# Bias of the first tiles summed ahead of their scores, masks made early, and a third buffer for the late loads

## The chip, the cores and the metric

The kernel runs on one core of a Trainium2 chip. The time is the device time of one execution in microseconds (us). A profile taken with an execution has a span, which is some 2 us shorter than the time. Most executions of one kernel agree within 0.3%; a few fall in a slower state, and those are left out of every ratio below. The verdict "same" means a difference of less than 2%. Where the text says faster or slower, it means only that the 95% interval of the ratio leaves out 1.

## The reference, cut to what matters

Attention with a local window and a few global keys, and behind it a layer with a squared ReLU:

```python
B, H, S, D = 4, 8, 768, 64            # 24 tiles of 128 rows
scores = q @ k.T / sqrt(D) + bias     # bias = -slope[h] * distance
keep   = (key < 8) | (0 <= row - key < 96)
a      = softmax(where(keep, scores, -1e9))
x      = (a @ v)                      # 3072 x 512 in all
out    = relu(x @ w_in) ** 2 @ w_out  # 512 -> 2048 -> 512
```

## The kernel before

It goes through 24 tiles of 128 rows. A tile's query and key are transposed (`tr`, copied to `qkT`), multiplied to scores (`sc`), put through exp on ScalarE (`at`), multiplied with the values (`po`), divided by the row sums to `x`, and transposed again (`trx`, copied to `xT`). Two tiles make a block of 256 rows; for each block come eight steps of `hT` (x @ w_in), ReLU and square, and `acc` (the product with w_out). For tiles from 6 on, SyncE's transposing DMAs take the place of `tr` and `trx`. A planner in the kernel's source simulates the engines with assumed durations and fixes the order of all instructions when the kernel is built; each engine then works through its own instructions in that order.

Three parts matter here. The first loads, on the queue of GpSimd, and the constants on VectorE:

```python
load_part(0, 1)                                   # q of tile 1
nc.gpsimd.iota(pbi, ...)                          # key minus row
load_part(1, 1); load_v(0); load_v(1)
# ...
nc.vector.tensor_tensor(out=pb, in0=pbt, in1=pbw, op=Alu.min)     # the bias
for h in range(H):
    nc.vector.tensor_scalar_mul(sid[h], ident, float(slopes[h] / scale))
def emit_pb0(e):                                  # the bias with global keys
    nc.vector.tensor_copy(pb0, pb[:, 0, :])
    nc.vector.tensor_scalar_max(pb0[:n_global, :], pb0[:n_global, :], float(-n_local))
# ...
for w in "i0 T2 i1 T3 i2 o0 i3 o1 i4 o2 T4 i5 o3 i6 o4 T5 i7 o5 o6 o7".split():
    ...                # T: q, k, v of a tile; i, o: a slice of w_in, of w_out
```

For tiles 0 to 2 the bias is added on TensorE: the scores open a sum, and a product of a scaled identity `sid` with `pb` closes it:

```python
for ...: nc.tensor.matmul(out=sc[odd, g][:, at, :], lhsT=qkT[...], rhs=qkT[...],
                          start=(odd, g) not in opened, stop=False)
for ...: nc.tensor.matmul(out=sc[odd, g][:, at, :], lhsT=sid[2 * pair + odd],
                          rhs=pb0 if first else pb[:, kt, :], start=False, stop=True)
```

The loads of tiles 6 to 23 ("late") share NQ = 2 buffers. GpSimd waits with each until the transpose out of the buffer is done.

Of the kernel before, what the change touches and what calls it, by code (L numbers as in the profile page):

```python
# [21 lines left out]
class Plan:  # L22
# [9 lines left out]
    LAG = {"PE": 0.25, "ACT": 0.15, "DVE": 0.12, "SP": 2.6, "POOLQ": 0.8, "DMAQ": 1.2, "DMA": 0.0}  # L32
# [67 lines left out]
def kernel(  # L100
# [11 lines left out]
    nc = tc.nc  # L112
# [26 lines left out]
    NQ, NKT = 2, 2 * TPB  # L139
# [31 lines left out]
    LEADS = {6: 10, 7: 10}  # L171
    NHS = 14
    E_AT = 14.0
    NWARM = 8
    LEAD = 12
# [65 lines left out]
    for j in range(NFIRST + 2):  # L241
        nc.vector.memset(v_sb[j][:, :, D : D + 1], 1.0)
    load_part(0, 1)
    nc.gpsimd.iota(pbi, pattern=[[-P, 2], [-1, P]], base=0, channel_multiplier=1)  # L244
    issue[0] += 0.4
# [9 lines left out]
    nc.vector.tensor_scalar(ident32, pbi[:, 0, :], 0.0, None, op0=Alu.is_equal)  # L255
    nc.vector.tensor_scalar(ident, pbi[:, 0, :], 0.0, None, op0=Alu.is_equal)
# [7 lines left out]
    )  # L264
    nc.vector.tensor_tensor(out=pb, in0=pbt, in1=pbw, op=Alu.min)
    for h in range(H):
        nc.vector.tensor_scalar_mul(sid[h], ident, float(slopes[h] / scale))

    def emit_pb0(e):
        nc.vector.tensor_copy(pb0, pb[:, 0, :])  # L270
        nc.vector.tensor_scalar_max(
            pb0[:n_global, :], pb0[:n_global, :], float(-n_local)
        )
        nc.vector.memset(pb[:n_global, 1, :], float(-n_local))

    pb_op = plan.op(("pb",), {"DVE": 0.75}, emit_pb0, key=-40.0)

    def emit_ones(e, js):
        for j in js:
            nc.vector.memset(v_sb[j][:, :, D : D + 1], 1.0)  # L280
# [22 lines left out]
    def any_copy(e, dst, src):  # L303
        if e == "ACT":
            nc.scalar.copy(dst, src)  # L305
        else:
            nc.vector.tensor_copy(dst, src)  # L307

    maskE = [
        plan.op(  # L310
            ("E", odd, g), {"ACT": 0.8}, key=0.3 + 2 * g + odd, ready=E_AT,
            emit=lambda e, odd=odd, g=g: [
                nc.scalar.activation(
                    E[:, odd, g, i], pb, Act.Exp, scale=float(slopes[4 * g + 2 * i + odd])
                )
                for i in range(2)
            ],
        )
        for g in range(2)
        for odd in range(2)  # L320
    ]

    def emit_E0(e, odd):
# [8 lines left out]
            ("E0", odd), {"DVE": 0.6}, emit=lambda e, odd=odd: emit_E0(e, odd), key=9 + odd,  # L332
            deps=[maskE[odd], maskE[2 + odd]],
# [7 lines left out]
    xT_op = {}  # L341
    xT_of = {}
# [3 lines left out]
    for j in range(NT):  # L346
# [6 lines left out]
        if j in late:  # L353
            def emit_load(e, j=j):
                load_tile(j)
            ld = plan.op(
                ("load", j), {"POOLQ": 2.6}, emit_load, deps=qk_users[slot(j)] + [ones[j]],
                key=base, ready=issue[0],
            )
            qk_users[slot(j)] = []  # L360
            ld = plan.op(("data", j), {"DMAQ": 2.7}, None, deps=[ld], key=base)
            land["q", j] = land["k", j] = land["v", j] = ld
# [6 lines left out]
        for n in range(2) if j < JQK else ():  # L369
            users = []  # L370

            def emit_tr(e, j=j, n=n, fp=fp):
                tr = ps_g.tile([P, NPAIR, P], FP32 if fp else BF16, name="tr", tag="g")
                src = plain[n, j] if fp else qk_ring[slot(j)][:, n, :]
                for pair in range(NPAIR):
                    nc.tensor.transpose(  # L376
                        out=tr[:, pair, :], in_=src[:, pair * P : (pair + 1) * P],
                        identity=ident32 if fp else ident,
                    )
                tiles["tr", n, j] = tr  # L380

            tr = plan.op(
                ("tr", n, j), {"PE": 0.5 if fp else 0.24}, emit_tr,
                deps=[land["qk"[n], j]], key=base, takes=(*G, [users]),
            )

            def emit_T(e, j=j, n=n, T_=T_):
                any_copy(e, T_[:, n], tiles.pop(("tr", n, j)))

            c = plan.op(  # L390
                ("T", n, j), {"DVE": 0.7 if fp else 0.43, "ACT": 0.57}, emit_T,
                deps=[tr] + ku, key=base + 0.1,
            )
            users += [tr, c]
            parts.append(c)
            if not fp:
                qk_users[slot(j)].append(tr)
        if j >= JQK:
            def emit_dT(e, j=j, T_=T_):
                nc.sync.dma_start_transpose(  # L400
                    out=T_.rearrange("p n a c -> p (n a) c"),
                    in_=qk_ring[slot(j)].rearrange("p n c -> p (n c)"),
                )

            T = plan.op(
                ("T", j), {"SP": 2.0}, emit_dT,
                deps=[land["q", j], land["k", j], xT_op[j - 3]] + ku, key=base - 6,
            )
            qk_users[slot(j)].append(T)
            parts = [T]  # L410
# [8 lines left out]
        def emit_sc(e, gs, j=j, first=first):  # L419
            sc = {}  # L420
            for g in gs:
                for odd in range(2):
                    sc[odd, g] = ps_g.tile([P, 4, P], FP32, name="sc", tag="g")
                    tiles["sc", j, odd, g] = sc[odd, g]
            todo = [
# [4 lines left out]
            todo = [x for x in todo if x[0] in gs]  # L430
            opened = set()
            for g, pair, at, kt in todo:
                for odd in range(2):
                    half = slice(odd * D, (odd + 1) * D)
                    nc.tensor.matmul(  # L435
                        out=sc[odd, g][:, at, :],
                        lhsT=qkT[(j - kt) % NKT][half, 1, pair, :],
                        rhs=qkT[j % NKT][half, 0, pair, :],

                        start=j >= NBIAS or (odd, g) not in opened,  # L440
                        stop=j >= NBIAS,
                        skip_group_check=True,
                    )
                    opened.add((odd, g))
            for g, pair, at, kt in todo if j < NBIAS else ():
                for odd in range(2):
                    nc.tensor.matmul(
                        out=sc[odd, g][:, at, :],
                        lhsT=sid[2 * pair + odd],
                        rhs=pb0 if first else pb[:, kt, :],  # L450
                        start=False,
                        stop=True,
                        skip_group_check=True,
                    )

        deps = list(parts)
        if j < NBIAS:
            deps.append(pb_op)
# [3 lines left out]
        for gs in [(0,), (1,)] if j < NSPLIT and not first else [tuple(range(groups))]:  # L462
            n = 8 * len(gs)
            o = plan.op(
                ("sc", j, gs[0]), {"PE": 0.25 + 0.029 * n + (0.056 * n if j < NBIAS else 0)},
                lambda e, gs=gs, f=emit_sc: f(e, gs), deps=deps, key=base + 1 + 2 * gs[0],
                takes=(*G, busers[2 * gs[0] : 2 * gs[-1] + 2]),
            )
            ku.append(o)
# [3 lines left out]
        for g in range(groups):  # L473
            for odd in range(2):
# [3 lines left out]
                def emit_exp(e, j=j, odd=odd, g=g):  # L478
# [11 lines left out]
                    ("exp", j, odd, g), {"ACT": 0.58}, emit_exp, deps=[s_[g]],  # L490
# [3 lines left out]
                users += [s_[g], x_]  # L494
# [6 lines left out]
                def emit_mul(e, j=j, odd=odd, g=g, first=first):  # L501
# [10 lines left out]
                    ("mul", j, odd, g), vec(0.38), emit_mul,  # L512
                    deps=[x_, maskE0[odd] if first else maskE[2 * g + odd]],
# [8 lines left out]
        if 1 <= t < TPB - 1:  # L522
            def emit_gk(e, j=j, t=t):
# [5 lines left out]
                ("gk", j), vec(0.17), emit_gk, deps=list(s_.values()), key=base + 4  # L529
# [7 lines left out]
        for hf in range(2):  # L537
# [34 lines left out]
            def emit_norm(e, j=j, hf=hf):  # L572
# [13 lines left out]
                ("norm", j, hf), vec(0.6), emit_norm,  # L586
# [6 lines left out]
        if 1 <= t < TPB - 1:  # L593
            def emit_gv(e, j=j, t=t):
# [3 lines left out]
                ("gv", j), vec(0.28), emit_gv, deps=[p_, norm[1]], key=base + 5  # L598
# [7 lines left out]
        if j < JX:  # L606
# [23 lines left out]
            c = plan.op(("xT", j), {"DVE": 0.43, "ACT": 0.57}, emit_xT, deps=[f_], key=base + 5.1, takes=xT_ring)  # L630
            users += [f_, c]
            xusers.append(f_)
        else:
# [8 lines left out]
            c = plan.op(("xT", j), {"SP": 1.3}, emit_xT, deps=norm, key=base + 5, takes=xT_ring)  # L642
# [4 lines left out]
        if tt == 1:  # L647
            c["deps"].append(xT_op[j - 1])
# [5 lines left out]
    for n, (blk, s) in enumerate(order1):  # L654
# [31 lines left out]
        r = plan.op(("relu", blk, s), {"ACT": 0.58}, emit_relu, deps=[a], key=n + 0.5, takes=("hr", 2, [rusers]))  # L686
# [10 lines left out]
        d = plan.op(("sq", blk, s), vec(0.68), emit_sq, deps=[r], key=n + 1.0, takes=("hs", NHS, [husers]))  # L697
# [11 lines left out]
    for blk in range(NBLK):  # L709
# [9 lines left out]
        for s, sub, half in order2:  # L719
# [29 lines left out]
            if s == NSTEP - 1:  # L749
                ousers = []  # L750

                def emit_o(e, blk=blk, sub=sub, half=half, cols=cols):
                    o_sb = work.tile([P, d_model], FP32, name="o", tag="o", bufs=4)
# [4 lines left out]
                    ("o", blk, sub), {"ACT": 0.57, "DVE": 0.62} if half is None else {"ACT": 0.37},  # L758
                    emit_o, deps=[o], key=8 * blk + s + 1.0, takes=("o", 4, [ousers]),
# [4 lines left out]
                def emit_st(e, blk=blk, sub=sub, half=half, cols=cols):  # L764
# [5 lines left out]

                st = plan.op(
                    ("st", blk, sub), {"SP": 0.4}, emit_st, deps=[ev],
                    key=8 * blk + s + 9.0,
                )
                ousers.append(st)

    for o in plan.run({"PE": 4.2, "DVE": 4.4, "ACT": 4.2, "DMAQ": issue[1]}):
# [37 lines left out]
```

## Time and profile before

| | before |
|---|---|
| time, fast runs | 215.96 us (215.77 to 216.22) |
| span | 213.9 us |
| TensorE busy, its weight loads | 96%, 66% |
| first real matmul, end of the last | 4.58, 210.80 us |
| last slice of w_in landed | 37.3 us |

TensorE's busy share hides what is lost, because the records of pipelined matmuls overlap. I use one measure throughout, the **stall**: at a moment t, t less 4.4 us less the work started by then, where each matmul counts as its distance between starts (0.109 us for hT, 0.2155 for acc, and so on, as in the prediction), and 4.4 us is a fixed point shortly before the first of them. The matmuls are counted by the starts of their weight loads, because in some traces 31 or 32 of the 1992 matmul records are missing and no weight load is. A stall that grows by 0.5 us between two moments means that TensorE lost 0.5 us there. Before, it stands at 1.47 us at 10 us, 3.68 at 18, 6.40 at 30 and 9.24 at 200: two thirds of what is lost is lost in the first 30 us.

### The profile page before, as it was taken

To read this page: it belongs to the slowest core of one execution; us is meant where nothing else is said; L and a number is where in the kernel's file an instruction comes from. 1 tells how busy PE (TensorE), PEld (TensorE's weight loads), DVE (VectorE), ACT (ScalarE), POOL (GpSimd) and SP (SyncE) were. 2 spreads that over 40 slices of the span, in tenths; PEclk is the share of its full clock that TensorE was granted. 3 is DMA by queue.
4 is the path that set the end of the run, shared out by engine and by line. 5 is a ranking of instruction groups with operands and counts; after the bars stand their busy time and mean duration, and the time that the engine had idled before them with its cause. 6 is when DMAs were issued, how large, how long until landed. Compare 5 with 4: busy or idle time off the path is not lost.

```text
span 213.9 us, 5031 instructions
## 1 busy us (share of the span) xinstructions
PE 206.2 (96%) x1992; PEld 141.8 (66%) x1992; DVE 141.9 (66%) x366; ACT 118.7 (55%) x218; POOL 74.1 (35%) x91
## 2 busy tenths in 40 slices
PE   7889899999999999999999999999999999999994
PEld 3676567657667767766767767666767767766773
DVE  5377948736688767756868768756867767744540
ACT  2698575714574845743845745743845745734441
POOL 7997577309044350418043143226113000000000
PEclk9999999999999999999999999999999999999999
DMA  9999999999999999999969969999989910310202
GB/s 129 150 164 200 179 196 183 175 209 111 162 199 116 228 129 93 171 138 111 198 85 91 183 118 95 167 124 109 184 128 82 174 26 3 123 25 3 98 0 98
DMA packets 113702, 27.58 MB, mean 129 GB/s; under 512 B 104336, under 2 KB 110736, under 8 KB 113680
## 3 DMA queue, kind: packets, MB, share of 16 engines
q0 software_dynamic: 79200, 13.37, 82.8%
q1 hardware_dynamic: 34480, 13.90, 32.9%
q8 instruction: 15, 0.25, 0.5%
q14 instruction: 7, 0.06, 0.1%
HBM read 27.26 MB, written 6.29 MB: 157 GB/s over the span
## 4 chain that ended last, share of the span: by engine, by line
PE 86%; DMA 7%; POOL 4%; issue 1%; DVE 0%; ACT 0%; POOLq 0%
PE hT L661 38%; PE acc L731 38%; PE sc L435 5%; PE po L550 5%; DMA win<-in_moe_w_in_dram 4%; DMA qk<-in_k_dram 3%; POOL qk L193 2%; POOL v L193 2%; POOL win L193 1%; PE tr L376 0%; PE trx L613 0%; DVE x L578 0%; ACT o L305 0%; POOL pbi L244 0%; DVE v L595 0%
## 5 line engine op out<-in xcount | busy, mean ns | idle before, releaser
L661 PE MATMUL hT<-xT,win 128*128 128x256 bf16 x768 | 99.0, 273 | 0.5 <-DMA win<-in_moe_w_in_dram 0.3
L731 PE MATMUL acc<-wout,hs 128*128 128x512 bf16 (+1 forms) x400 | 95.6, 370 | 0.7 <-DMA wout<-in_moe_w_out_dram 0.7
L682 ACT ACTIVATE hr<-hT 128x512 f32<-128x512 f32 x96 | 57.3, 598 | 60.5 <-PE hT L661 58.9
L661 PEld LDWEIGHTS <-win 128*128 128x128 bf16 x768 | 71.0, 98 | 18.2 <-DMA win<-in_moe_w_in_dram 1.1
L694 DVE TENSOR_TENSOR hs<-hr 128x512 bf16<-128x512 f32 x96 | 65.0, 689 | 24.9 <-ACT hr L682 24.1
L731 PEld LDWEIGHTS <-hs 128*128 128x128 bf16 x400 | 38.4, 98 | 28.5 <-issue 0.8
L483 ACT ACTIVATE esc<-sc 128x512 bf16<-128x512 f32 x78 | 42.6, 598 | 13.2 <-PE sc L435 13.1
L193 POOL DMA_DIRECT2D qk<-in_q_dram x23 | 20.6, 897 | 82.5 <-DMA qkT<-qk 79.5
L508 DVE TENSOR_TENSOR at<-esc,E 128x512 bf16<-128x512 bf16 x78 | 32.4, 420 | 6.8 <-ACT esc L483 5.8
L193 POOL DMA_DIRECT2D v<-in_v_dram x24 | 21.6, 901 | 2.2 <-DVE at L508 1.2
L578 DVE TENSOR_TENSOR x<-po,rs 128x256 bf16<-128x256 f32 x48 | 20.4, 424 | 1.7
L193 POOL DMA_DIRECT2D qk<-in_k_dram x23 | 20.6, 897 | 0.2 <-issue 0.2
L550 PEld LDWEIGHTS <-at 128*128 128x128 bf16 x352 | 16.7, 98 | 5.8 <-ACT at L483 0.4
L550 PE MATMUL po<-v,at 128*128 128x65 bf16 x352 | 18.7, 193 | 0.3 <-ACT at L483 0.3
L435 PEld LDWEIGHTS <-qkT 64*128 64x128 bf16 x352 | 9.9, 94 | 9.9 <-issue 8.3
L577 DVE RECIPROCAL rs<-po 128x4 f32<-128x4 f32 x48 | 8.6, 179 | 10.2 <-PE po L550 10.2
L435 PE MATMUL sc<-qkT 64*128 64x128 bf16 x192 | 13.2, 219 | 1.0 <-DVE qkT L307 0.5
L305 ACT COPY o<-acc 128x512 f32<-128x512 f32 (+1 forms) x14 | 7.8, 557 | 9.2 <-PE acc L731 9.2
L307 DVE COPY o<-acc 128x512 f32<-128x512 f32 x11 | 7.6, 691 | 6.1 <-PE acc L731 6.1
L435 PE MATMUL sc<-qkT,qkT 64*128 64x128 bf16 x160 | 11.4, 216 | 0.0
L524 DVE COPY qkT<-qkT 128x32 bf16<-128x32 bf16 x16 | 3.8, 235 | 7.4 <-PE sc L435 7.3
L193 POOL DMA_DIRECT2D win<-in_moe_w_in_dram x8 | 6.7, 840 | 0.6 <-DMA wout<-in_moe_w_out_dram 0.6
(40 smaller groups left out, 61.3 us busy)
## 6 DMA issues: line engine op xcount, KB each, us to landing
out_dram<-o SPq DMA_DIRECT2D x23, 256.0 KB, 4.1
v<-in_v_dram POOLq DMA_DIRECT2D x24, 128.0 KB, 6.0
qk<-in_q_dram POOLq DMA_DIRECT2D x23, 128.0 KB, 4.5
qk<-in_k_dram POOLq DMA_DIRECT2D x23, 128.0 KB, 5.4
win<-in_moe_w_in_dram POOLq DMA_DIRECT2D x8, 256.0 KB, 8.1
wout<-in_moe_w_out_dram POOLq DMA_DIRECT2D x8, 256.0 KB, 8.9
qkT<-qk SPq DMA_TRANSPOSE x18, 5.1
xT<-x SPq DMA_TRANSPOSE x18, 3.5
```

The costliest lines, as they stand in the source:

```text
L193: nc.gpsimd.dma_start(out=dst, in_=src)
L305: nc.scalar.copy(dst, src)
L435: nc.tensor.matmul(out=sc[odd, g][:, at, :], lhsT=qkT[(j - kt) % NKT][half, 1, pair, :], rhs=qkT[j % NKT][half, 0, pair, :],  start=j >= N ...
L483: nc.scalar.activation(out=esc, in_=tiles.pop(("sc", j, odd, g)).rearrange("p a c -> p (a c)"), func=Act.Exp, scale=scale,)
L508: nc.vector.tensor_mul(at, tiles.pop(("esc", j, odd, g)), bias)
L550: nc.tensor.matmul(out=po[:, hi, :], lhsT=tiles["at", j, odd, g][:, at * P : (at + 1) * P], rhs=v_sb[kj][:, h, :], start=(i == 0), stop=(i ...
L577: nc.vector.reciprocal(rs, po[:, :, D : D + 1])
L578: nc.vector.tensor_tensor(out=x[:, 4 * hf : 4 * hf + 4, :], in0=po[:, :, :D], in1=rs.to_broadcast([P, 4, D]), op=Alu.mult,)
L661: nc.tensor.matmul(out=hT[:, c, :], lhsT=w_in_sb[s][:, kt, c * P : (c + 1) * P], rhs=tiles["xT", blk][:, kt, :], start=(kt == 0), stop=(kt ...
L682: nc.scalar.activation(hr, tiles.pop(("hT", blk, s)), Act.Relu)
L694: nc.vector.tensor_mul(hs, hr, hr)
L731: nc.tensor.matmul(out=tiles["acc", blk, sub, half], lhsT=hs[:, c, sub * P : (sub + 1) * P], rhs=w_out_sb[s][:, c, cols], start=(s == 0 an ...
```

## The change

Its intent is to shorten the front: the bias opens the sum and needs no query, so it can be computed while the copies of the query and key run; the masks `E` are made while ScalarE has nothing else; a third late buffer lets loads be issued earlier, and a small memset on VectorE (the gate) takes GpSimd's wait for the transpose. The planner also gets durations closer to measured ones. The diff, cut to its core:

```diff
-    NQ, NKT = 2, 2 * TPB
+    NQ, NKT = 3, 2 * TPB
...
+    nc.gpsimd.iota(pbi, ...)
     load_part(0, 1)
-    nc.gpsimd.iota(pbi, ...)
     load_part(1, 1)
     load_v(0)
...
     nc.vector.tensor_tensor(out=pb, in0=pbt, in1=pbw, op=Alu.min)
+    nc.vector.tensor_copy(pb0, pb[:, 0, :])
+    nc.vector.memset(pb[:n_global, 1, :], float(-n_local))
+    nc.vector.tensor_scalar_max(pb0[:n_global, :], pb0[:n_global, :], float(-n_local))
     for h in range(H):
         nc.vector.tensor_scalar_mul(sid[h], ident, float(slopes[h] / scale))
+    for ...:                                      # 8 masks, now ahead of all exps
+        nc.scalar.activation(E[:, odd, g, i], pb, Act.Exp, scale=...)
...
+    gate = plan.op(("gate", j), {"DVE": 0.07},
+        memset of qk_ring[slot(j)][:, :, :1], deps=qk_users[slot(j)] + [ld, xT_sp.get(j - 3)])
-    ld = plan.op(("load", j), ..., deps=qk_users[slot(j)] + [ones[j]])
+    ld = plan.op(("load", j), ..., deps=qk_users[slot(j)] + [ones[j], gate])
...
+    bias = plan.op(("bias", j, gs[0]), ..., deps=[tr])        # start=True, stop=False
+    o = plan.op(("sc", j, gs[0]), ..., deps=[*deps, bias])    # start=False, stop=True
...
-    LAG = {"PE": 0.25, "ACT": 0.15, "DVE": 0.12, "SP": 2.6, ...}
+    LAG = {"PE": 0.25, "ACT": 0.26, "DVE": 0.2, "SP": 0.6, ...}
     # and some ten durations of single operations, and planned entries for the
    # transfers of transposes and stores; on VectorE the identities move behind pbt and pbw
```

## The prediction

> **What bounds the kernel now.** I read the page first: busy shares, then the 40 slices.
>
> ```profile
> span 213.9 us, 5031 instructions
> PE 206.2 (96%) x1992; PEld 141.8 (66%) x1992; DVE 141.9 (66%) x366; ACT 118.7 (55%) x218; POOL 74.1 (35%) x91
> ...
> PE   7889899999999999999999999999999999999994
> ...
> DMA  9999999999999999999969969999989910310202
> ```
>
> The reader sees a TensorE that is never clearly idle after slice 7 (5.35 us each), and DMA engines that are full from the first slice. PE busy at 96% is not yet a bound, because busy spans of pipelined matmuls overlap. So I took the distance between starts instead. The chain of waits in order of time shows it in the steady part:
>
> ```profile
> 45.63 0.86 PE acc L731 x4
> 46.49 0.87 PE hT L661 x8
> ```
>
> A group of 4 acc matmuls advances TensorE by 0.86 us (0.216 each), a group of 8 hT by 0.87 (0.109 each); in the same view 16 score matmuls take 0.55 and 16 po matmuls 0.48; from starts in the timeline a 128-column bias or bf16 transpose takes 0.056 and an fp32 transpose 0.213. The streaming work is then 768 x 0.109 = 83.5, 368 x 0.2155 + 32 x 0.109 = 82.8, scores 22 x 0.55 = 12.1, po 22 x 0.48 = 10.6, bias 40 x 0.056 = 2.3, transposes 64 x 0.057 + 8 x 0.213 = 5.3: 196.6 us. The first real matmul starts at 4.58 and the last one ends at 210.80 (3.1 before the end), so 206.2 us are there for 196.6 of work: 9.6 us of stall in all. Adding up, in the timeline, every start minus (previous start + its interval), about 6.5 us of this lie between 5 and 30 us and under 3 us in the 170 us after 38, there almost all as 0.1 us where the kind of matmul changes. **The kernel is bound by TensorE from about 30 us on; only the first 30 us have anything to give.** There the timeline names two kinds of stall. First a latency chain (copy, score, exp, product, transpose) of tiles 0 to 2:
>
> ```profile
> 7.03 0.40 PE L435 MATMUL sc<-qkT 64*128 64x128 bf16 x8 [0.46 <-ACT qkT L305]
> 7.36 0.62 PE L447 MATMUL sc<-pb,sid 128*128 128x128 bf16 x8
> 7.81 0.39 PE L376 MATMUL tr<-ident,qk 128*128 128x128 bf16 x4
> 7.96 1.08 ACT L483 ACTIVATE at<-sc 128x512 bf16<-128x512 f32 x2 [0.99 <-PE sc L447]
> 8.72 0.23 PE L435 MATMUL sc<-qkT 64*128 64x128 bf16 x2 [0.52 <-DVE qkT L307]
> ...
> 9.65 2.23 ACT L483 ACTIVATE at<-sc 128x512 bf16<-128x512 f32 x4 [0.60 <-PE sc L447]
> ...
> 13.02 0.28 PE L613 MATMUL trx<-ident,x 128*128 128x128 bf16 x2 [0.40 <-DVE x L578]
> 13.03 1.33 ACT L313 ACTIVATE E<-pb 128x256 bf16<-128x256 bf16 x4
> ```
>
> In starts these are 0.62 (at 7.03), 0.68 (8.72), 0.42 (11.93) and 0.56 (13.02): 2.3 us. Then waits for landings:
>
> ```profile
> 23.88 1.05 PE L661 MATMUL hT<-xT,win 128*128 128x256 bf16 x8 [0.32 <-DMA win<-in_moe_w_in_dram]
> 24.76 0.41 PE L550 MATMUL po<-v,at 128*128 128x65 bf16 x8
> 25.91 1.02 PE L731 MATMUL acc<-wout,hs 128*128 128x512 bf16 x4 [0.74 <-DMA wout<-in_moe_w_out_dram]
> ```
>
> With 16.56, 27.40, 27.90 and 29.62 they make 0.55 + 0.49 + 0.90 + 0.19 + 0.26 + 0.30 = 2.7 us. The rest are 0.1 us changes of kind.
>
> **What the Trainium skill says.** The page "Perfetto Trace Analysis", in its section "Identifying the Most-Contended Engine", calls matmul occupancy a poor measure of the distance to the roofline and takes the weight-load share instead. The trace agrees: PE 96% against PEld 66%, and 9.6 us of stall are in the span although only about 4 us show as idle. "TensorE: Matmul & The Clock Gate", section "Wait — 56ns, not 53.3ns?", gives 55.6 ns between starts of warm 128-column matmuls and 215.7 ns of 512-column ones; the medians here are 56 and 216 ns, so nothing in the matmuls themselves can be gained. "DMA: Bandwidth & Descriptors", section "Issuing engines are not separate DMA queues", says that all issuers share 16 engines; here the landings come at an even pace from 5 to 46 us (about 0.86 us for a 128 KB part of a tile, 1.3 us for a 256 KB weight slice) whether GpSimd issues without pause or waits, so the pace of the engines sets the landings, not the issue.
>
> **The change part by part.**
> (a) Bias ahead of scores. Same 40 matmuls of 0.056, moved. For tile 0 its 8 (0.45 us) no longer stand between 7.35 and 7.80 but fit into the gap from 6.41 (end of the transpose at 6.18) to 7.03. The first exp goes from 7.96 to about 7.5. The transpose of the key of tile 1 (landed 6.70, held until 7.81 only by the order on TensorE) goes to about 7.36; its copy (0.42 plus latencies, 0.91 from 7.81 to 8.72) lets the scores of tile 1 start at 8.27 with the bias already summed: 0.25 us later they are done, 8.5 against 9.50 before. The four exps follow at 0.56 each, so the last ends near 10.9 instead of 11.88, and all behind it (po, division, transpose at 13.02, first hT at 14.91) can come **about 1.0 us earlier**.
> (b) Masks early. 8 ACT instructions of 0.33 us = 2.7 us leave 13.03, 18.92 and 21.98, where they stand among exps and relus of tiles 2 and 3, and go to ACT's idle time before 5.68, where pb is ready. DVE work before pb is 0.42 + 0.32 + 0.23 + 0.22 + 0.42 = 1.6 us after an iota that now comes first (about 1.2 instead of 2.72), so pb at about 3, pb's memset 3.3, masks done at 6.0. ACT's first cast began at 5.68; up to 0.3 us of collision, which DVE can take over (its own work, 8 sid of 0.17 included, ends near 5). Gain **0.3 us**, at tile 2.
> (c) Iota ahead of the first load: the load goes back by 0.37 us at most, the next one not at all; the engines are then busy with the two 256 KB fp32 loads from SyncE. **Zero**, +-0.2.
> (d) Third late buffer and gates. 16 memsets (tiles 8 to 23) of about 0.1 us, an estimate from the smallest VectorE pieces here (0.17): 1.6 us on an engine that is 66% busy. GpSimd now waits 79.5 us in total for transposes; this becomes a wait for the memset. Loads go earlier by up to a tile. All of it lies after 40 us, where TensorE waits for no transfer: **zero**.
> (e) Corrected durations in the planner (relu 0.48 for 0.58, square 0.61 for 0.68, others) change the static order on all engines. It could hide some of the 2.7 us of landing stalls. I grant 0.5 us.
>
> **How much of it can stay.** The weights' landings are not moved, so what is gained by 15 us can be lost again waiting at 23.88 or 29.62. What could be done before the last win slice (lands 37.32)? Attention of tiles 0 to 5: 1.7 + 2.3 + 3.0 + 2.6 + 2.3 + 1.4 = 13.3 us; hT of blocks 0 and 1 with seven slices 14 x 0.87 = 12.2; acc with five wout slices 5 x 0.86 = 4.3: 29.8, so 4.58 + 29.8 = 34.4 against 37.32. Done by then today: 37.3 - 4.6 - 6.9 of stall = 25.8. Up to 4 us of work is there to fill in, about 3 after the changes of kind. So the gain is not barred, but the order is fixed at build time and must use it. I take 1.0 + 0.3 + 0.5 = 1.8 and give 0.3 back to landings: **-1.5 us, 214.4 us**.
>
> **The rivals.** (1) The landing takes the place of the latency: TensorE arrives 1.3 us earlier at 23.88 and waits 1.3 us longer. For it: four waits in a row end with a landing, and in the chain 20.40 to 29.57 is all one transfer. Against: the 4 us of spare work above. It would leave 215.5 to 216. (2) The gate blocks VectorE: a memset at the head of its in-order queue waits for a transpose that takes 5.1 us to land, squares behind it come late and TensorE starves. Against: three tiles lie between load and transpose, and 14 hs buffers are ahead. It would cost some 0.3 us per tile, to 219 at the worst. (3) The new order uses the landings better than I grant, all of the 3 us: 213. (4) More loads in flight delay the xT transposes (3.5 us now) in the steady part; they would show as TensorE waits after 40 us and make 216 or more.
>
> **Range and chances.** From full use (-3.2) to rival 1 with a little harm (+0.2): 212.8 to 216.1. Two per cent is 4.3 us, more than the spare work allows, so faster by over 2% has 0.04; slower by over 2% needs rival 2 or 4 in strength, 0.03.
>
> **What would show it.** Right: sid matmuls ahead of the scores between 6.3 and 7.1; exps of tile 1 ending near 10.9; transpose of tile 1's x near 12.0; E on ACT before 6; win landings within 0.3 us of before; the steady part, from 45 us on, with only 0.1 us gaps. Rival 1: idle at win or wout grown by over 1 us. Rival 2: VectorE idle before the gate memsets and TensorE idle behind hs. Wrong altogether if the landings move by over 1 us, or if stalls after 40 us change by over 1 us.

## The result, and the profile after

A ratio here is the mean time of one kernel's fast runs over the mean of the other's fast runs of the same rounds; it is not quite the ratio of the medians quoted beside it. Medians here are of fast runs.

| | before | after |
|---|---|---|
| time, median (range) | 215.96 (215.77 to 216.22; a fourth run, 220.68, was slow) | 215.09 (214.93 to 215.44) |
| ratio, 95% interval | | 0.9961 (0.9941 to 0.9981) |
| span | 213.9 | 213.1 |

By the ratio the change gains 0.8 us of the predicted 1.5, with an interval of 0.4 to 1.3. The page of the kernel after, the lines that answer to those shown of before (busy times, and the share of each fortieth of the span in tenths):

```profile
span 213.1 us, 5046 instructions
...
PE 205.5 (96%) x1992; PEld 141.2 (66%) x1992; DVE 142.4 (67%) x383; ACT 117.5 (55%) x217; POOL 74.4 (35%) x91
...
PE   7968999999999999999999999999999999999994
...
DMA  9999999999899999999999899799999992310202
```

The reader sees one new dip, a 6 in the third slice (10.7 to 16.0 us), where before had 8. The timeline of TensorE shows what is in it; first the kernel before, from 11 us on (start, length, and in brackets idle time and what ended it):

```profile
11.93 0.35 PE L550 MATMUL po<-v,at 128*128 128x65 bf16 x6 [0.25 <-ACT at L483]
12.12 0.39 PE L376 MATMUL tr<-ident,qk 128*128 128x128 bf16 x4
12.34 0.28 PE L613 MATMUL trx<-ident,x 128*128 128x128 bf16 x2
...
14.91 1.04 PE L661 MATMUL hT<-xT,win 128*128 128x256 bf16 x8
```

And after, from the scores of tile 0 on:

```profile
6.49 0.40 PE L449 MATMUL sc<-qkT 64*128 64x128 bf16 x8
6.92 0.40 PE L372 MATMUL tr<-ident,qk 128*128 128x128 bf16 x4
7.16 0.61 PE L433 MATMUL sc<-pb,sid 128*128 128x128 bf16 x8
...
10.56 0.36 PE L562 MATMUL po<-v,at 128*128 128x65 bf16 x6 [0.26 <-ACT at L495]
11.99 0.40 PE L372 MATMUL tr<-ident,qk 128*128 128x128 bf16 x4 [1.08 <-DMA qk<-in_q_dram]
12.87 0.40 PE L372 MATMUL tr<-ident,qk 128*128 128x128 bf16 x4 [0.48 <-DMA qk<-in_k_dram]
13.11 0.61 PE L433 MATMUL sc<-pb,sid 128*128 128x128 bf16 x8
13.55 0.39 PE L625 MATMUL trx<-ident,x 128*128 128x128 bf16 x4
...
14.87 1.05 PE L675 MATMUL hT<-xT,win 128*128 128x256 bf16 x8
```

The latency chain did become shorter: the last po of tile 1 starts at 10.56 instead of 11.93. But then TensorE waits 1.08 us for the query of tile 2 and 0.48 us for its key, and the first hT comes at 14.87, where it was at 14.91. The stall tells the same in numbers:

| stall at (us) | 10 | 12 | 18 | 24 | 30 | 60 | 200 |
|---|---|---|---|---|---|---|---|
| before | 1.47 | 2.18 | 3.68 | 4.69 | 6.40 | 7.13 | 9.24 |
| after | 0.55 | 2.26 | 3.74 | 5.21 | 5.75 | 6.35 | 8.37 |

At 10 us the change is 0.92 us ahead; at 12 us all of it is gone; at 24 us it is 0.52 behind; by 30 us it is 0.65 ahead, since between 24 and 30 us it loses 0.54 where the kernel before loses 1.71, in good part in waits for weights, and that is nearly all that is left at the end. What is left was thus not gained where the prediction put most of it. The landings show what is waited for: the query of tile 2 landed at 11.95 instead of 11.13, its key at 12.83 instead of 11.99, the first slice of w_in at 11.09 instead of 10.29, the last at 38.12 instead of 37.32. Even without that delay little could have been kept at this place: in the kernel before, TensorE started on tile 2's key at 12.12, only 0.13 us after it had landed. **The whole schedule of landings came 0.8 us later**, which the prediction had excluded. The issues on GpSimd show where that starts. Before (the last line is the first slice of w_in):

```profile
2.35 0.37 POOL L244 IOTA pbi<- 128x256 int32 x1
2.64 0.95 POOL L193 DMA_DIRECT2D qk<-in_k_dram  x1
3.59 1.75 POOL L193 DMA_DIRECT2D v<-in_v_dram  x2
5.32 0.77 POOL L193 DMA_DIRECT2D win<-in_moe_w_in_dram  x1
```

And after:

```profile
2.35 0.89 POOL L193 DMA_DIRECT2D qk<-in_k_dram  x1
3.22 2.37 POOL L193 DMA_DIRECT2D v<-in_v_dram  x2
5.57 0.77 POOL L193 DMA_DIRECT2D win<-in_moe_w_in_dram  x1
```

The two loads of values take 2.37 us to issue instead of 1.75. Taken singly, the first goes from 3.22 to 4.72, 1.50 us where before had 0.88; the second is unchanged at 0.88. So the issues, 0.37 us ahead at 3.22 because the iota has moved, are 0.25 us behind at 5.57.

In the steady part the change does what its text says and no more. GpSimd's waits stand in the page in the group of the query loads (instructions, then busy time and mean ns, then idle time before them and what ended most of it); before:

```profile
L193 POOL DMA_DIRECT2D qk<-in_q_dram x23 | 20.6, 897 | 82.5 <-DMA qkT<-qk 79.5
```

And after:

```profile
L193 POOL DMA_DIRECT2D qk<-in_q_dram x23 | 20.6, 894 | 87.0 <-DVE qk L346 75.0
```

GpSimd now waits 75.0 us for the gate on VectorE instead of 79.5 us for the transpose, and from 60 us to 200 us TensorE loses 2.02 us (2.11 before).

### The profile page after: what moved, and what is told of

It reads as the page before. It is cut to its first block, busy times and chain, and to the rows that moved or that the text cites. A ratio compares the mean times of both kernels' runs of the same rounds, so it can differ in the third digit from the quotient of the medians.

```text
span 213.1 us, 5046 instructions
## 1 busy us (share of the span) xinstructions
PE 205.5 (96%) x1992; PEld 141.2 (66%) x1992; DVE 142.4 (67%) x383; ACT 117.5 (55%) x217; POOL 74.4 (35%) x91
## 3 DMA queue, kind: packets, MB, share of 16 engines
HBM read 27.26 MB, written 6.29 MB: 157 GB/s over the span
## 4 chain that ended last, share of the span: by engine, by line
PE 87%; DMA 7%; POOL 4%; issue 0%; ACT 0%; POOLq 0%
PE hT L675 39%; PE acc L745 38%; DMA win<-in_moe_w_in_dram 7%; PE sc L449 5%; PE po L562 4%; POOL qk L193 2%; POOL v L193 1%; PE tr L372 0%; POOL win L193 0%; PE trx L625 0%; ACT o L304 0%; POOL pbi L246 0%; POOLq L246 0%; POOLq L813 0%
## 5 line engine op out<-in xcount | busy, mean ns | idle before, releaser
L745 PE MATMUL acc<-wout,hs 128*128 128x512 bf16 (+1 forms) x400 | 98.1, 371 | 0.2 <-DMA wout<-in_moe_w_out_dram 0.2
L675 PEld LDWEIGHTS <-win 128*128 128x128 bf16 x768 | 72.8, 98 | 23.9 <-DMA win<-in_moe_w_in_dram 1.6
L708 DVE TENSOR_TENSOR hs<-hr 128x512 bf16<-128x512 f32 x96 | 65.9, 687 | 23.0 <-ACT hr L696 21.7
L745 PEld LDWEIGHTS <-hs 128*128 128x128 bf16 x400 | 36.5, 98 | 24.4 <-issue 0.4
L495 ACT ACTIVATE esc<-sc 128x512 bf16<-128x512 f32 x78 | 42.1, 601 | 10.3 <-PE sc L449 10.3
L193 POOL DMA_DIRECT2D v<-in_v_dram x24 | 22.2, 924 | 2.4 <-DVE at L520 1.2
L495 ACT ACTIVATE at<-sc 128x512 bf16<-128x512 f32 x10 | 5.3, 598 | 2.5 <-PE sc L449 2.5
```

The source lines that it names most:

```text
L193: nc.gpsimd.dma_start(out=dst, in_=src)
L495: nc.scalar.activation(out=esc, in_=tiles.pop(("sc", j, odd, g)).rearrange("p a c -> p (a c)"), func=Act.Exp, scale=scale,)
L675: nc.tensor.matmul(out=hT[:, c, :], lhsT=w_in_sb[s][:, kt, c * P : (c + 1) * P], rhs=tiles["xT", blk][:, kt, :], start=(kt == 0), stop=(kt ...
L708: nc.vector.tensor_mul(hs, hr, hr)
L745: nc.tensor.matmul(out=tiles["acc", blk, sub, half], lhsT=hs[:, c, sub * P : (sub + 1) * P], rhs=w_out_sb[s][:, c, cols], start=(s == 0 an ...
```

## The experiments

Theory A at the start: the front's gain is real and is eaten by landings that come later because of the issue on GpSimd. Rival B: the static order on TensorE throws the gain away (the transposes of tile 2 stand in front of those of tile 1's x, which were ready earlier). Rival C: the landings would have eaten it anyhow, held issue or not. Rival D: the gain comes from the third buffer, not the front. All kernels gave correct results, apart from two that leave loads out on purpose.

### Both kernels again

> The kernel before, unchanged, for a second trace. Question: are the landings of the loads the same from run to run? If the 0.8 us by which the landings from the first win slice on came later in the changed kernel is chance, they should scatter by as much here (first win 10.29, tile 2 q 11.13, last win 37.32 in the first trace). If it belongs to the change, they stay within 0.2 us.

> The changed kernel, unchanged, for a second trace and a better time. Theory (the change itself moves the landings): first win near 11.1, tile 2 q near 11.95, last win near 38.1 again, time 215.0 to 215.2. Rival (chance): landings back near 10.3, 11.1 and 37.3 and then TensorE less held at 12 us.

The kernel before took 216.02 us in its one look; the kernel after 215.00 (214.46 to 215.67), ratio 0.9917 (0.9877 to 0.9957). That ratio, 1.8 us, shows more gain than the medians do, because four of the kernel before's ten fast runs on this chip lay between 217.3 and 218.1. With the repeat on another chip below (0.9936, or 1.4 us) the change is worth 0.8 to 1.8 us, and in both repeats the predicted 1.5 lies inside the interval: that half of the gain is missing holds for the first comparison, and how much is missing is not settled. In the trace of the kernel before, the first slice of w_in landed at 10.95 where it had landed at 10.29: **the landings of one and the same kernel scatter by about 0.65 us** (in two executions), so a single trace can't settle a difference of that size. The issue did not scatter: 1.50 us again after.

### The iota first, alone

```diff
+    nc.gpsimd.iota(pbi, ...)
     load_part(0, 1)
-    nc.gpsimd.iota(pbi, ...)
```

> The kernel before with only the iota put ahead of the first load; planner and order of TensorE unchanged. If the earlier iota makes the landings late, by itself or by pulling VectorE work (sid, bias) under the issue of the first v load, first win lands 0.5 to 0.8 us later (near 10.9 to 11.1) and the time is the same or up to 0.5 us longer. If the late landings come from other parts (masks on ACT, gates), they stay within 0.2 us of the kernel before.

215.56 us (214.97 to 218.13, one slow run left out), ratio 0.9948 (0.9903 to 0.9993). The issue of the first v stayed at 0.90 us and the first slice of w_in landed at 10.29, as before. So the place of the iota is not what moved the landings, nor is it enough that VectorE's products come earlier: here they start at 2.83; whether it is worth something by itself the wide interval leaves open. Its trace fell on a run of 218.13 us and shows something else, told below with b_bias.

### Another order on TensorE

```diff
-                deps=[land["qk"[n], j]], key=base, takes=(*G, [users]),
+                deps=[land["qk"[n], j], trx_ops.get(j - 1) if j == 2 else None],
+                key=base, takes=(*G, [users]),
...
+    # and the transpose of tile 2's key behind the first hT group
```

> The changed kernel with two more edges in the planner: transposes of tile 2 behind the transpose of tile 1's output, and the k transpose of tile 2 behind the first hT group. Theory (the gain of the front was lost because the fixed order on TensorE put transposes of tile 2, whose data landed at 11.95 and 12.83, ahead of work that was ready): hT starts near 12.4 instead of 14.87 and the time falls by 0.5 to 0.9 us, to 214.2 to 214.6. Rival (later landings of win and wout take every gain back): hT starts early but waits at win and wout grow as much and the time stays within 0.3 us of 215.1.

The order came out as meant. The timeline of TensorE in this kernel:

```profile
11.62 0.29 PE L627 MATMUL trx<-ident,x 128*128 128x128 bf16 x2 [0.49 <-DVE x L592]
11.96 0.40 PE L373 MATMUL tr<-ident,qk 128*128 128x128 bf16 x4
12.51 1.03 PE L678 MATMUL hT<-xT,win 128*128 128x256 bf16 x8
...
15.85 0.40 PE L373 MATMUL tr<-ident,qk 128*128 128x128 bf16 x4 [0.63 <-DMA qk<-in_q_dram]
16.69 0.40 PE L373 MATMUL tr<-ident,qk 128*128 128x128 bf16 x4 [0.45 <-DMA qk<-in_k_dram]
```

The first hT starts at 12.51, 2.4 us earlier than in either kernel, and yet the time is 215.13 us (214.70 to 215.81), the same as after: what was gained at 12 us is waited for at 15.85 and 16.69, where the next tile's query and key land. At 18 us the stall is 3.74, as in after. Rival B falls as the cause of the loss: with another order the same time is waited for at other landings. The last slice of w_in landed at 37.07 in this trace, although the issue of the first v was held (1.50 us).

### Loads left out, with a wrong result

To see how far landings set the front, the loads of v of tiles 1 to 3 are left out (tile 0's values stand in), before and after:

```diff
+        if j in (1, 2, 3):
+            land["v", j] = land["v", 0]
+            return
```

> The kernel before without the loads of v of tiles 1 to 3 (they use v of tile 0; wrong result on purpose). Theory (from 11 to 24 us the landings set how far TensorE can be): the landings behind them come up to 2.9 us earlier, and the stall by 20 us falls from 4.1 us to about 3, the time by about 1 us to 215. Rival (the chain of copies, exps and orders is what holds TensorE in the front): no more than 0.3 us.

> The changed kernel without the same three loads (wrong result on purpose). Theory (landings took the front's gain): with the landings out of the way more of the 0.9 us that it leads by at 10 us is kept, so it is faster than b_nov by 1.3 to 1.7 us, against 0.85 with all loads. Rival (the gain was lost to the order of TensorE alone): the difference stays at 0.8 to 0.9.

Before: 213.77 us (213.49 to 214.01), ratio 0.9887 (0.9859 to 0.9914), so 2.4 us less for three loads of some 0.9 us of transfer each (the pace of the landings); about 1 us had been expected. The front is bound by landings, for most of the 2.7 us of transfer counts. After: 213.28 us (213.16 to 213.60). The change is worth only 0.5 us here, where 1.3 to 1.7 were expected: a miss. The held issue was there in a_nov too (1.50 us), and its first slice of w_in landed at 10.38 against 9.48, so this pair doesn't free the change from what held it back, as I had thought it would.

### The values one transfer later

```diff
-    for w in "i0 T2 i1 T3 i2 o0 i3 o1 i4 o2 T4 i5 o3 i6 o4 T5 i7 o5 o6 o7".split():
+    for w in "i0 Q2 i1 V2 Q3 i2 V3 o0 i3 o1 i4 o2 Q4 i5 V4 o3 i6 o4 Q5 i7 V5 o5 o6 o7".split():
```

> The changed kernel with each v of tiles 2 to 5 loaded one transfer later (behind a weight slice or the q and k of the next tile), all the same bytes. Theory (landings set the pace to 24 us, and v is the one that is needed last): k of tile 3 and win slices 1 and 2 land about 1 us earlier, the stall by 20 us falls by 0.5 us or more, the time to 214.2 to 214.7. Rival: no change within 0.2 us of 215.0.

215.34 us (214.49 to 216.98), ratio 0.9965 (0.9928 to 1.0003): no gain, a miss. The landings did come as expected: slices 1 and 2 of w_in (counted from 0) at 14.44 and 18.33 (16.09 and 19.94 in after), the last at 36.50. But the stall at 20 us was 5.4, not 0.5 below the 4.5 of after: the query of tile 2, which stands ahead of the moved loads, still landed at 12.04 and was waited for, and tile 2's v now landed at 15.82 (13.80). Earlier weights, paid for with a later v, are thus worth nothing here.

### The third buffer and the gates, alone

Only NQ = 3 and the gate are put into the kernel before.

> The kernel before with only the three late buffers and the gates. Theory (they act only after 40 us, by keeping the loads off the xT transposes): best runs stay within 0.3 us of 216.0, but the runs at 217 to 218 in the fast state, which the kernel before shows and the changed kernel does not, are gone; no wait of TensorE for xT in the trace. Rival (the slow runs come from the chip and not from the loads): they show up here as often.

216.22 us (215.95 to 216.58), ratio 1.0000 (0.9974 to 1.0025). Rival D falls: the third buffer is worth nothing to the median. None of its six runs was over 216.6, while the kernel before on the same chip reached 217.35, but in one of eleven, so six runs say little of that.

### The bias ahead, alone

The split of bias and scores (the last part of the diff above) in the kernel before, with its two buffers, its late masks and its planner.

> The kernel before with only the bias matmuls taken out of the scores and put ahead of them; masks, VectorE's order at the start, planner's times and buffers as before. By the prediction's working this part is 1.0 us of the front: exps of tile 1 end near 10.9. If its gain is kept where landings are not late: time 215.0 to 215.4, about the same as the whole change. If landings take it as well: stall by 18 to 20 us within 0.3 us of before and time 215.6 to 216.0.

217.67 us (217.18 to 219.48), ratio 1.0058 (1.0011 to 1.0106): **slower**. The front's gain is there at 10 us (a stall of 0.55, exactly as after) and gone at 12 (2.09; before 2.18), although the issue of the first v is not held here (0.88 us). TensorE waits for tile 2's query and key, as after:

```profile
10.68 0.35 PE L565 MATMUL po<-v,at 128*128 128x65 bf16 x6 [0.25 <-ACT at L498]
11.84 0.40 PE L376 MATMUL tr<-ident,qk 128*128 128x128 bf16 x4 [0.80 <-DMA qk<-in_q_dram]
12.66 0.40 PE L376 MATMUL tr<-ident,qk 128*128 128x128 bf16 x4 [0.43 <-DMA qk<-in_k_dram]
```

The stall at 30 and 60 us is 6.62 and 7.24, where the two traces of the kernel before have 6.40 and 6.62, then 7.13 and 7.35. So landings take the whole gain of this part, as the second half of the expectation had it. This is one trace, with tile 2's query at 11.79, which is within the scatter of the kernel before (11.13 and 11.80). What makes the time worse lies far behind the front. TensorE's waits in this kernel (total, times, longest):

```profile
PE hT L676 <- DMA xT<-x: 2.0, 1, 2.0
PE acc L746 <- DMA wout<-in_moe_w_out_dram: 1.2, 2, 0.9
```

The first is a single wait at 70.69 us for the transposing DMA of tile 7's x. The trace of b_iota (its run of 218.13 us) has the same wait, in the timeline of TensorE:

```profile
70.66 1.05 PE L661 MATMUL hT<-xT,win 128*128 128x256 bf16 x8 [2.25 <-DMA xT<-x]
```

There that transpose was issued at 64.30 us and landed at 70.61, 6.3 us, beside late loads issued from 63.20 to 65.80. In the kernel before it was issued at 64.46 and landed at 68.08, 0.33 us before the matmuls that need it start. None of the traces with three buffers has this wait. My reading, argued and not shown, since no run changes the transpose alone: with two buffers the late loads bunch beside that transpose, and a small shift tips it into a wait of 2 us; this is the tail of the kernel before, and the third buffer with its gates takes the tail away without making the best runs faster.

### The held issue: VectorE operations that don't hold it

What runs on VectorE while the first v is issued are mainly the eight scaled identities. The view of that tile in the kernel before (durations in ns, least, median, most; first and last start):

```profile
L267 DVE TENSOR_SCALAR sid<-ident x8: 175/331/586, 4.1 to 4.9; 128x128 bf16<-128x128 bf16 x8
```

And in the kernel after:

```profile
L273 DVE TENSOR_SCALAR sid<-ident x8: 175/176/585, 3.4 to 4.1; 128x128 bf16<-128x128 bf16 x8
```

Before, the products start at 4.06, when the issue of the first v (3.59 to 4.47) has begun, and it is they that wait: their median is 331 ns, the issue takes 0.88 us. After, the global rows' bias and the products start at 2.81 and 3.40, and the issue (3.22 to 4.72) is the one that waits: seven products take 0.176 us each, and the last, which takes 0.585, ends with it within 0.02 us. The Trainium skill has the mechanism in its page "SBUF — State Buffer", section "Who interferes with whom": VectorE in a mode that uses both of its port pairs and GpSimd share one pair as an exclusive lock, `copy` and `tensor_scalar` can enter such a mode, a DMA issued by GpSimd needs the pair to write its descriptors, and "Issue order, not op shape, decides who blocks." The traces agree that either side can wait for the other, with the numbers above. The order of the starts in the trace does not tell which: in b_iota the products start at 2.83, ahead of the same issue at 3.22, and they wait (434 and 594 ns the longest) while the issue takes 0.90 us. Why the issue loses in the one kernel and wins in the other stays open.

A kernel to test it: the same values in the kernel after by `scalar_tensor_tensor`, with two inputs in SBUF, a form that was expected not to hold the issue.

```diff
-    nc.vector.tensor_copy(pb0, pb[:, 0, :])
+    stt(out=pb0, in0=pb[:, 0, :], scalar=0.0, in1=pb[:, 0, :], op0=Alu.min, op1=Alu.min)
-    nc.vector.tensor_scalar_max(pb0[:n_global, :], pb0[:n_global, :], float(-n_local))
+    stt(out=pb0[:n_global, :], in0=pb0[:n_global, :], scalar=float(-n_local),
+        in1=pb0[:n_global, :], op0=Alu.max, op1=Alu.max)
     for h in range(H):
-        nc.vector.tensor_scalar_mul(sid[h], ident, float(slopes[h] / scale))
+        stt(out=sid[h], in0=ident, scalar=float(slopes[h] / scale), in1=ident,
+            op0=Alu.mult, op1=Alu.mult)
```

> The changed kernel with pb0, its maximum and the eight sid made by an instruction with two inputs in SBUF instead of copies and products with one input; same values, same place in the order. Theory (these VectorE instructions hold GpSimd off while it writes the descriptors of the first v load: in five of five traces of the changed kind that issue takes 1.50 us and ends 0.02 us after the last sid, against 0.88 to 0.90 in five of five of the kind before): the issue takes about 0.9 us, the first win slice lands near 10.4 instead of 11.1 to 11.5, the stall by 14 us falls by 0.4 us or more and the time to 214.2 to 214.7. Rival (the masks on ACT or chance hold the issue): it takes 1.5 us still, landings and time as in the changed kernel.

214.08 us (213.59 to 214.57), ratio 0.9882 (0.9841 to 0.9924): faster than the kernel before, and by its median than the kernel after. The chip was another than that of a2, so the pair was run again, together, and with a control: the same edit in the kernel before, where no issue was held.

> The changed kernel again, beside a_lock2 on one chip, so that the two can be compared in the same rounds. Both theories: 215.0 to 215.6; the issue of the first v load on GpSimd 1.50 us, the first win slice down at 11.1 to 11.6.

> a_lock again, on the chip of a3. Theory (the issue of the first v load on GpSimd is held by VectorE's scaled identities and the landings behind it come later): issue 0.9 us, first win slice at 10.4 to 10.7, 0.6 to 1.0 us faster than a3. Rival (the gain of a_lock was its chip's or chance): within 0.4 us of a3.

> Control: the kernel before with the same two-input forms of the scaled identities and of the global rows' bias. Theory: GpSimd was not held there (issue 0.88 us), so the landings do not move (first win slice 10.3 to 10.9) and the time stays within 0.4 us of before. Rival (the two-input form itself is what made a_lock faster, whatever the landings): 0.6 us or more faster than before.

| one chip | median (range) | ratio to before, 95% interval |
|---|---|---|
| before | 216.00 (215.31 to 218.09) | |
| after (a3) | 215.00 (214.06 to 217.03) | 0.9936 (0.9898 to 0.9975) |
| after, edited (a_lock2) | 213.96 (213.56 to 214.32) | 0.9897 (0.9864 to 0.9930) |
| before, edited (b_lock) | 216.10 (215.71 to 218.21, two slow runs left out) | 1.0018 (0.9966 to 1.0070) |

The edit is worth 1.0 us in the kernel after by the medians (0.8 by the two ratios, whose intervals overlap), and nothing in the kernel before. The issue and the products in the trace of a_lock2:

```profile
3.22 1.77 POOL L193 DMA_DIRECT2D v<-in_v_dram  x2
4.95 0.79 POOL L193 DMA_DIRECT2D win<-in_moe_w_in_dram  x1
```

```profile
L277 DVE SCALAR_TENSOR_TENSOR sid<-ident x8: 271/273/274, 3.3 to 4.8; 128x128 bf16<-128x128 bf16 x8
```

Each product is slower (273 ns for 176), yet none waits, and the two issues take 1.77 us as they did before. The part of the expectation that failed is a landing: in this trace the first slice of w_in came at 11.11 and not at 10.4 to 10.7 (10.50 in a_lock). All landings up to tile 2's v (13.81) are in fact those of after (13.80), and TensorE still waits at 12.85 for the key of tile 2; only the second slice of w_in (slice 1) is earlier, at 14.99 instead of 16.09:

```profile
12.85 0.40 PE L379 MATMUL tr<-ident,qk 128*128 128x128 bf16 x4 [0.45 <-DMA qk<-in_k_dram]
```

The scatter of 0.65 us is as large as the effect, so the landings are compared over all traces of a kind:

| | issue of first v | first w_in slice landed | last w_in slice landed | stall at 30 us |
|---|---|---|---|---|
| before, b2, b_lock | 0.88 | 10.29, 10.95, 10.74 | 37.32, 37.51, 37.40 | 6.40, 6.62, 6.83 |
| after, a2, a3 | 1.50 | 11.09, 11.52, 11.26 | 38.12, 38.51, 38.40 | 5.75, 6.29, 7.72 |
| a_lock, a_lock2 | 0.89 | 10.50, 11.11 | 36.44, 37.38 | 4.11, 4.87 |

By the last slice the two traces of the edited kernel are 0.7 us or more ahead of every trace of the unedited one, and the stall at 30 us has fallen by 0.9 to 3.6 us (the 3.6 rests on a3, whose trace fell on its longest run, 217.03). But a landing of the last slice does not fix the time: a_fill and a_vlate have 37.07 and 36.50 and no gain. Where the stall grows says more:

| stall | at 10 us | at 12 us | grows from 12 to 24 | from 24 to 30 |
|---|---|---|---|---|
| before, b2 | 1.47, 1.72 | 2.18, 2.33 | 2.51, 2.70 | 1.71, 1.59 |
| b_bias | 0.55 | 2.09 | 2.76 | 1.77 |
| after, a2, a3 | 0.55, 1.03, 0.79 | 2.26, 2.32, 2.32 | 2.95, 3.54, 5.05 | 0.54, 0.44, 0.36 |
| a_lock, a_lock2 | 0.50, 1.10 | 2.09, 2.27 | 1.92, 2.40 | 0.10, 0.21 |

So Rival C is half right. What the bias gains by 10 us is gone at 12 us in every trace, whether the issue is held or not. What the held issue costs comes mostly from 12 to 24 us, and what the change gains for good comes from 24 to 30 us, where b_bias shows nothing of it. Theory A holds for the cost of the held issue and not for the bias.

### The held issue doubled, and the edit with the other order

A second, unused set of eight products in the kernel after doubles what holds the issue.

```diff
+    for h in range(H):
+        nc.vector.tensor_scalar_mul(sid2[h], ident, float(slopes[h] / scale))
```

> The changed kernel with a second set of eight sid products behind the first, which nobody reads: the suspected hold on GpSimd doubled, 0.8 us more of VectorE. Theory: the issue of the first or second v load ends 0.4 to 0.8 us later again (5.1 to 5.5, or 6.2 for the second), the first win slice lands near 11.8, time 215.3 to 215.7. Rival: issue and landings as in the changed kernel; time moved by 0.2 us at most.

The issue of the first v grew to 2.32 us and ended with the last product of the second set, again within 0.02 us, so it is these products that hold it. In the first 9 us the DMA engines moved 118 GB/s, where the five traces with an issue of 1.50 us and tile loads left whole have 127 to 133 and the nine with an issue of 0.90 us or less 132 to 142. The timeline of GpSimd:

```profile
3.22 3.20 POOL L194 DMA_DIRECT2D v<-in_v_dram  x2
6.38 0.78 POOL L194 DMA_DIRECT2D win<-in_moe_w_in_dram  x1
```

The first slice of w_in landed at 11.75. The time did not follow: 215.14 us (214.31 to 216.79), as after, and the last slice of w_in landed at 38.21, where the three traces of after have 38.12 to 38.51. So 0.2 to 0.7 us of the delay of 0.8 reach the first slice, with a scatter as large, and nothing the last; the cost of a held issue is not in proportion to its length, and why the second 0.8 us was made up for stays open.

Last, the edit together with the other order on TensorE:

> Both edits: sid and pb0 made as in the run before, and the transposes of tile 2 behind tile 1's output and the first hT group. Theory (landings decide): equal to the run before within 0.3 us, since an earlier hT only moves the wait to the next landing. Rival (order and landings each hold a part): faster than it by 0.4 us or more.

215.10 us (214.22 to 215.82), ratio 0.9925 (0.9881 to 0.9969): 1.0 us worse than a_lock on the same chip. The issue was 0.9 us, the last slice of w_in landed at 37.66 in its trace, and the stall at 30 us was 6.07. It was expected to equal a_lock within 0.3 us or to beat it, so both the theory and its rival missed. In a_fill the order cost nothing, here it costs what the edit gives: with this order the free issue is worth nothing (215.13 held, 215.10 free, on two chips). I have no shown cause for that.

## Why the prediction was right or wrong

The time of 215.09 us lies within the range, and "same" was the likely verdict, but in the first comparison about half the gain is missing, and the sum came that near partly by luck: two of its steps failed, each by about 1 us, and another term was worth more than was granted.

- **(a) Bias ahead: right for the chain, and the first step that failed for what is kept.** The exps of tile 1 end at 10.50 (10.9 was predicted, 11.88 before), and the stall at 10 us fell by 0.92 us. But "all behind it [...] can come **about 1.0 us earlier**", with 0.3 given "back to landings", did not come true: the transpose of tile 1's x is at 13.55 (near 12.0 was the sign of being right, 13.02 before), the first hT at 14.87 (14.91), and at 12 us nothing of the gain is left. b_bias shows that this part alone, with the issue not held, loses it all in the same way (a stall of 2.09 at 12 us, 6.62 at 30). The waits that ended there were for the query and key of tile 2.
- **(b) Masks early: right in place.** E is made on ScalarE from 3.32 to 5.88 us. Its 0.3 us can't be told from the rest.
- **(c) is the second step that failed:** "Iota ahead of the first load: the load goes back by 0.37 us at most, the next one not at all [...] **Zero**, +-0.2", and with it "The weights' landings are not moved" and "the pace of the engines sets the landings, not the issue". The iota itself is indeed worth nothing in landings (b_iota). But in the new order of VectorE's work the bias and the eight products hold the issue of the first v: 1.50 us instead of 0.88, and in this trace landings 0.8 us later from the first slice to the last. I looked at what each engine does and not at what VectorE does to GpSimd. The term is mis-sized by about 1.0 us of the final time: that is what a_lock2 gains over a3 side by side on one chip, while b_lock gains nothing over before; on another chip a_lock was at 214.08. Without the held issue the same change gives 214.0 us, 0.4 below the predicted time.
- **(d) Third buffer and gates, zero: right for the median** (b_gate, 1.0000). What it may do for the slowest fast runs was not foreseen.
- **(e) Planner, 0.5 us: not separated, and with (b) too small.** With (a) kept at nothing and (c) at -1.0, the 2.0 us by which a_lock2 is ahead of before are left to (b) and (e), if the parts add up, which no run tests. The traces put 1.2 us of it between 24 and 30 us, where the stall grows by 0.54 in after and by 1.71 before: there the waits for w_in and w_out, which the prediction had at 2.7 us from 16 to 30, are mostly gone. Neither the bias (b_bias, 1.77) nor the third buffer (b_gate, 1.92) does that.
- **"How much of it can stay"** looked only at the last slice of w_in, where there is spare work. It should have looked at the first landings: the query and key of tile 2 at 12 us, and the loads that b_nov shows to count almost one for one.
- **Rivals.** Rival 1 (a landing takes the latency's place) came true, not at 23.88 as expected but at 11.99 and 12.87, and in b_bias and a_lock with the issue free too. Rival 2 didn't: the gates block nothing. Rival 4 didn't either; I take the late transposes to be at more risk with two buffers than with three, as argued above and not shown.

Open: what the held issue does between its end and the later landings, and why it costs about 1.0 us in the change's order and nothing in the other; why a doubled hold cost no more than a single one; what decides whether the issue or the products wait; whether (b) or (e) made the gain from 24 to 30 us; and what makes the landings of one kernel scatter by 0.65 us. That the bias's gain goes to landings is shown by b_bias, and that the held issue costs about 1.0 us in this kernel by the edit and its control; the law by which a hold turns into time is not shown.

## What to carry to other kernels

Before moving work on VectorE to an earlier time, look at what GpSimd is issuing then: copies and scalar products in SBUF can hold the issue of a load (1.50 us instead of 0.88 here), and what lands behind it can come later. When the front is bound by landings, ask of each microsecond gained what the next thing to land is, and look at every landing that TensorE waits for, not at the last alone. And run the same kernel twice before reading a landing: here a difference of 0.6 us in one trace means nothing.

## What the Trainium skill lacked or had wrong

- "SBUF — State Buffer", section "Who interferes with whom", says that the one who comes second is blocked for the whole instruction. The runs show that a series holds for longer than one instruction: eight products back to back, all but the last of 0.176 us, held the issue for 0.6 us (1.50 for 0.88), sixteen for 1.4 us (2.32), until the last one. The page has figures for a DMA beside a single `tensor_copy`, none for a series.
- The same section doesn't say how a trace shows which side came first. The order of the starts did not tell it here: products that start ahead of the issue waited in b_iota (2.83 against 3.22, issue 0.90 us), and in after products that start behind it (3.40) held it (1.50 us).
- The same page lists `copy`, `cast` and `tensor_scalar` as those that take the shared pair and `tensor_tensor` as harmless to descriptor generation ("inferred"). It doesn't name `scalar_tensor_tensor` (its rule for two inputs in SBUF covers only GpSimd's reads); here eight of them, of 0.273 us each with both inputs in SBUF, left the issue at 0.89 us in two traces.
- I found no page that gives the scatter of landings between executions of one program: 0.65 us at the first weight slice here (10.29 and 10.95), with equal issue times.
